# Weight blocks A for batches 0 and 1, then B for 1 and 0, with a second buffer of split inputs that attention fills directly

## The chip, the cores and the metric

The kernel runs on one core of a Trainium2 chip. The metric is the device time of one execution in microseconds (us), the median of several runs. In the texts below PE is TensorE (matmul), ACT is ScalarE, DVE is VectorE, SP is SyncE, which here only issues DMAs.

## What is computed

Three stages follow each other, all in float32, over 4 batches of 8 heads, 512 local and 32 global positions, 64 columns a head.

```
k_all, v_all = concat(k_g, k_l), concat(v_g, v_l)
out_g = softmax(q_g k_all^T / 8) v_all                      # 32 global rows see everything
out_l = softmax([q_l k_g^T / 8, band(q_l k_l^T / 8)]) v_all  # 512 local rows: global + |i-j| <= 32
x = concat(out_g, out_l) -> (4*544, 512)
x = (silu(x @ w_gate) * (x @ w_val)) @ w_out                # 512 -> 1536 -> 512: "layer 1"
h = x @ w_in;  x = (max(h,0) + alpha*min(h,0)) @ w_out2     # 512 -> 2048 -> 512: "layer 2"
```

The weights arrive as pairs of float32 words read as 64-bit integers, so each block has to be taken apart on the chip.

## The kernel before

Everything that TensorE does in the two layers runs on numbers split into a high and a low part, each of a rounded 32-bit type: three matmuls (high·high, high·low, low·high) stand for one. `mm12` (line 460) is such a product over a contraction of 512: 4 pieces by 3 passes, 12 matmuls. `xa` holds the split inputs of layer 1 and later of layer 2.

**Attention** is cut into 40 units (`Local`: two heads, 256 query rows; `Global`: four heads), 4 steps each, run by `apump` (line 317): scores on PE, masked minimum on DVE, exponentials on ACT (`s`), division on DVE (`n`), transposes on PE with a copy by ACT (`t`), the product with V on PE and its copy out (`pv`). A step of one unit stands beside steps of its neighbours, so a unit's chain is spread over three rounds. In the opening stretch a step may use any of 8 PSUM banks; afterwards only the two banks `a0` and `a1` (line 651). `pv` writes batch 0's result split into `xa` (two instructions, lines 222 and 223); of batches 1 to 3 it writes the result unsplit into `yp` or `y3`, by one ACT copy (line 219).

**Weights.** `wload` issues the DMA of a block, `wpump` converts one in seven instructions: lines 407, 408 and 424 on ACT (424 in some cases as line 422 on DVE), lines 409, 410, 413 and 388 on DVE. The 36 blocks of layer 1 (12 slices `f` of gate, value and out) are split once, written back to HBM as `w1s`, and read again as `w<-w1s` when they are wanted a second time. SBUF holds 18 blocks of layer 1: the half GA (f 0 to 5) or the half GB (f 6 to 11). `reload` queues the blocks of the other half one by one as those of this half are used for the last time.

**Visits.** `visit1(b, c0, c1, fs, ...)` runs columns c0 to c1 of batch b through one half of the slices: per slice 12 matmuls for gate (`ps_g`), 12 for value (`ps_v`), 12 for out (`ps_acc`). Before the first visit 24 attention steps run with no layer work beside them (the opening). The order then is, with the short names used below:

- 0a: batch 0, columns 0 to 255, GA; 0b: batch 0, columns 256 to 511, GA
- 0GB, 1GB, 1GA, 2GA, 2GB: a whole batch (512 columns) through one half
- 3: batch 3 and the global rows, in four visits; then layer 2 in five chunks (`visit2`)

What interleaves them is `pump()`: called several times in a visit, it starts `wrate` weight loads, takes one conversion step, and runs attention steps until their count has reached its share of a target (`pumper`: `nslots` calls to reach `target`). So the numbers ns0 to ns3 say how thickly attention stands in each visit, and ws1 how many weight loads go with each step of the opening. At the end of a visit `xprep` splits the next batch's `yp` into `xa` (`yprep`), and the same is done between the chunks of layer 2, by `boundary`.

The recording layer then places each engine's instructions in an order of its own from the program order and dependencies, so that neighbours in the code may stand some places apart on an engine.

Of the kernel before, what the change touches and what calls it, by code (L numbers as in the profile page):

```python
# [39 lines left out]
def kernel(  # L40
# [303 lines left out]
    st["w"], st["lo"] = 0, 0  # L344
# [4 lines left out]
    def dbl_tile():  # L349
        i = ring["d"] = (ring["d"] + 1) % ND  # L350
        if i == 2 and st["k"] < mark[3] - 4:
            return const.tile([128, 512], I64, tag="y30", name="dblx")
# [42 lines left out]
    def wpump():  # L395
# [60 lines left out]
    def xprep(b):  # L456
        assert st["k"] >= mark[b + 1] + LAG
        yprep(b, 0, S)

    def mm12(o, w, c0, c1):  # L460
# [96 lines left out]
    def yprep(b, c0, c1):  # L557
        for k in range(4):
            if (c0, c1) == (0, S) and b < B - 1:
                src = yp[b][:, :, k]  # L560
                hi, lo = (xa[:, i, k, 0:S].rearrange("p (a c) -> p a c", a=2) for i in range(2))
                with pr("xp"):
                    nc.scalar.activation(out=hi, in_=src, func=ACTF.Copy)
                    nc.vector.tensor_tensor(out=lo, in0=src, in1=hi, op=ALU.subtract)
                continue
            for src, o, z in ypieces(b, c0, c1):
                hi, lo = xa[:, 0, k, o:o + z], xa[:, 1, k, o:o + z]
                nc.scalar.activation(out=hi, in_=src(k), func=ACTF.Copy)
                nc.vector.tensor_tensor(out=lo, in0=src(k), in1=hi, op=ALU.subtract)
# [8 lines left out]
    def visit2(b, c0, c1, pump, late, alpha, boundary=None):  # L578
# [15 lines left out]
        for f in range(NF2):  # L594
# [33 lines left out]
    if True:  # L628
# [95 lines left out]
        chunks = [(0, 0, 512), (1, 0, 512), (2, 0, 512), (3, 0, 384), (3, 384, 640)]  # L724
        for i, (b, c0, c1) in enumerate(chunks):
            nx = chunks[i + 1] if i + 1 < len(chunks) else None
            visit2(b, c0, c1, p, late, alpha, boundary=(lambda nx=nx: yprep(*nx)) if nx else None)
# [84 lines left out]
```

## Time and profile before

| | |
|---|---|
| runs | 988.06 us median of 3 (986.29 to 989.24) |
| the profiled execution | 986.18 us; its span, first to last instruction, 984.4 us |
| PE busy | 965.3 us (98%), mean granted clock 0.989 |
| ACT busy, DVE busy | 488.2 us (50%), 522.3 us (53%) |
| DMA | 103.43 MB, 105 GB/s over the span |

A busy share over the whole span hides that the first fifth and the rest are different: in the first 175 us ACT and DVE are busy nine tenths of the time, afterwards a quarter to a half. PE's matmuls are pipelined and their ends are modelled, so PE reads as busy even where it advances slowly; the number of matmuls that a stretch holds says more. The rows below are therefore cut at the borders of the visits.

### The profile page before, as it was taken

The page shows a single profiled execution, that of the slowest core. Times are in us where ns is not written, and L with a number is a line of the kernel's source. Part 1 is how long each engine was busy: PE and PEld are TensorE (multiplying, and loading weights), DVE is VectorE, ACT ScalarE, POOL GpSimd, SP SyncE. Part 2 cuts the span into 40 slices and gives each one's busy share as a digit, 9 for nine tenths or more (in the row PEclk, how much of TensorE's full clock was granted, in tenths as well). Part 3 has the DMA queues.
Part 4 walks back from the last instruction along what each step waited for, and adds up shares of the span by engine and source line. Part 5 has one row for each costly group of instructions (what it writes and reads, how often), then busy time and mean ns, then how long its engine had stood idle before and what let it go on. Part 6 is the DMA issues. An engine that isn't in the chain of part 4 may idle for free.

```text
span 984.4 us, 14324 instructions
## 1 busy us (share of the span) xinstructions
PE 965.3 (98%) x5556; PEld 801.5 (81%) x5556; DVE 522.3 (53%) x1247; ACT 488.2 (50%) x983; POOL 0.7 (0%) x6
## 2 busy tenths in 40 slices
PE   7899999999999999999999999999999999999998
PEld 5678887777777777778999998888888888899897
DVE  6889888553323443325941279944434543444453
ACT  7899999755565655653532155523222322322322
POOL 0000000000000000000000000000000000000000
PEclk9699999999999999999999999999999999999999
DMA  8979795425421034401368033200100100010000
GB/s 262 321 260 338 230 345 161 172 70 182 148 90 50 28 103 132 150 1 55 120 207 254 10 108 129 86 1 1 43 1 1 43 1 1 0 43 1 8 26 21
DMA packets 33683, 103.43 MB, mean 105 GB/s; under 512 B 3920, under 2 KB 8016, under 8 KB 33616
## 3 DMA queue, kind: packets, MB, share of 16 engines
q1 hardware_dynamic: 33616, 102.53, 31.5%
q8 instruction: 43, 0.70, 0.3%
q14 instruction: 24, 0.20, 0.1%
HBM read 79.18 MB, written 23.33 MB: 104 GB/s over the span
## 4 chain that ended last, share of the span: by engine, by line
PE 83%; DVE 7%; ACT 5%; DMA 4%; issue 1%; SPq 0%; ACTq 0%; DVEq 0%
PE ps_acc L590 19%; PE ps_g L466 17%; PE ps_v L466 16%; PE ps_acc L499 10%; PE ps_a L466 9%; PE ps_a L157 3%; DMA dbl<-in_w_dram 3%; PE ps_a L211 3%; PE ps_a L203 2%; DVE raw L413 1%; DVE dbl L410 1%; PE ps_a L240 1%; PE ps_a L283 1%; DVE w L388 1%; ACT e L183 1%
## 5 line engine op out<-in xcount | busy, mean ns | idle before, releaser
L466 PE MATMUL ps_g<-xa,w 128*128 128x512 f32 (+2 forms) x1032 | 210.6, 352 | 0.9 <-ACT sg L513 0.9
L466 PE MATMUL ps_v<-xa,w 128*128 128x512 f32 (+2 forms) x1032 | 208.9, 351 | 0.5 <-DVE w L388 0.5
L466 PEld LDWEIGHTS ps_g<-xa,w 128*128 128x128 f32 x1032 | 168.9, 190 | 30.2 <-issue 8.4
L466 PEld LDWEIGHTS ps_v<-xa,w 128*128 128x128 f32 x1032 | 169.1, 190 | 24.9 <-issue 4.7
L590 PE MATMUL ps_acc<-w,h 128*128 128x512 f32 x561 | 138.2, 392 | 0.2 <-DVE h L609 0.2
L590 PEld LDWEIGHTS ps_acc<-w,h 128*128 128x128 f32 x561 | 104.5, 188 | 22.5 <-DVE h L609 0.6
L499 PE MATMUL ps_acc<-h,w 128*128 128x512 f32 (+2 forms) x600 | 119.5, 351 | 0.0
L499 PEld LDWEIGHTS ps_acc<-h,w 128*128 128x128 f32 x600 | 97.4, 189 | 15.2 <-issue 2.7
L522 DVE TENSOR_TENSOR t<-ps_v,sg 128x512 f32<-128x512 f32 (+1 forms) x54 | 35.7, 660 | 124.0 <-PE ps_v L466 106.1
L466 PE MATMUL ps_a<-xa,w 128*128 128x512 f32 (+2 forms) x480 | 100.8, 359 | 0.0
L466 PEld LDWEIGHTS ps_a<-xa,w 128*128 128x128 f32 x480 | 83.5, 188 | 13.4
L170 DVE CUSTOM_DVE_ANT_0 e<-ps_a,lm 128x256 f32<-128x256 f32 x112 | 41.7, 421 | 56.8 <-PE ps_a L157 56.5
L183 ACT ACTIVATE e<-e,mx 128x256 f32<-128x256 f32 x128 | 63.7, 499 | 14.9 <-DVE mx L170 13.8
L608 ACT ACTIVATE h<-g 128x512 fp32r<-128x512 f32 (+2 forms) x55 | 31.3, 568 | 74.4 <-DVE g L607 74.4
L590 PE MATMUL ps_acc<-w,hx 128*128 128x512 f32 x255 | 63.1, 394 | 0.0
L604 DVE TENSOR_SCALAR g<-ps_a,alpha 128x512 f32<-128x512 f32 (+2 forms) x40 | 26.8, 671 | 57.6 <-ACT r L603 57.1
L590 PEld LDWEIGHTS ps_acc<-w,hx 128*128 128x128 f32 x255 | 47.5, 188 | 10.4
L513 ACT ACTIVATE sg<-ps_g 128x512 f32<-128x512 f32 (+1 forms) x54 | 31.0, 574 | 46.4 <-PE ps_g L466 46.1
L513 ACT ACT_TABLE_LOAD x30 | 38.5, 1283 | 28.6 <-PE ps_g L466 28.3
L603 ACT ACTIVATE r<-ps_a 128x512 f32<-128x512 f32 (+2 forms) x40 | 21.2, 531 | 59.0 <-PE ps_a L466 58.6
L609 DVE TENSOR_TENSOR h<-g,h 128x512 fp32r<-128x512 f32 (+2 forms) x55 | 33.7, 612 | 31.1 <-ACT h L608 31.0
L607 DVE TENSOR_TENSOR g<-g,r 128x512 f32<-128x512 f32 (+2 forms) x80 | 48.9, 611 | 2.4
(123 smaller groups left out, 1071.9 us busy)
## 6 DMA issues: line engine op xcount, KB each, us to landing
w<-w1s SPq DMA_DIRECT2D x54, 512.0 KB, 3.6
dbl<-in_w_dram SPq DMA_DIRECT2D x50, 512.0 KB, 4.0
w1s<-w SPq DMA_DIRECT2D x36, 512.0 KB, 5.2
qk<-in_qk_dram SPq DMA_DIRECT2D x12, 592.0 KB, 5.8
dblx<-in_w_dram SPq DMA_DIRECT2D x9, 512.0 KB, 5.6
yp<-in_w_dram SPq DMA_DIRECT2D x9, 512.0 KB, 6.1
out_dram<-o SPq DMA_DIRECT2D x16, 256.0 KB, 2.0
v<-in_v_dram SPq DMA_DIRECT2D x12, 320.0 KB, 4.2
```

The source lines that it names most:

```text
L157: nc.tensor.matmul(out=s[h][:, 256 * i:256 * i + 256], lhsT=x[rows, WIN + 128 * t:WIN + 128 * t + 128], rhs=x[rows, 128 * t:128 * t + 256] ...
L170: nc.vector.tensor_tensor_reduce(out=self.e[:, j], in0=s[h][:, 256 * i:256 * i + 256], in1=lm[:, 2 * self.half + i], scale=-0.125, scalar= ...
L183: nc.scalar.activation(out=self.e[:, j], in_=self.e[:, j], func=ACTF.Exp, scale=-1.0, bias=mx[:, j:j + 1], accum_out=self.sm[:, j:j + 1],)
L211: nc.tensor.matmul(out=o[D * h:D * h + D, c0:c1], lhsT=v[:, h, kt + d], rhs=self.pt[:, h, x:x + c1 - c0], start=(i == 0), stop=(i == 2),)
L466: nc.tensor.matmul(out=o, lhsT=a, rhs=x, start=(i == 0), stop=(i == 11))
L499: nc.tensor.matmul(out=acc[m][:, 0:n], lhsT=a, rhs=x, start=(f == fs[0] and j == 0), stop=(f == fs[-1] and j == 2),)
L513: nc.scalar.activation(out=sg[:, 0:nn], in_=g[:, 0:nn], func=ACTF.Silu)
L522: nc.vector.tensor_tensor(out=t[:, 0:nn], in0=v[:, 0:nn], in1=sg[:, 0:nn], op=ALU.mult)
L590: nc.tensor.matmul(out=acc[t], lhsT=a, rhs=x, start=(i == 0 and j == 0), stop=(i == NF2 - 1 and j == 2))
L607: nc.vector.tensor_tensor(out=g[:, 0:n], in0=g[:, 0:n], in1=r[:, 0:n], op=ALU.add)
L608: nc.scalar.activation(out=h[:, 0, 0:n], in_=g[:, 0:n], func=ACTF.Copy)
L609: nc.vector.tensor_tensor(out=h[:, 1, 0:n], in0=g[:, 0:n], in1=h[:, 0, 0:n], op=ALU.subtract)
```

## The change

- The order of visits becomes 0a, 0b, then 1GA, 1GB, 0GB, 2GB, 2GA, and in 3 the halves are swapped. GA so serves batches 0 and 1 before GB is wanted at all, and layer 1's blocks are read back from HBM in two visits and no longer in three.
- A second buffer `xb` (16 KB a partition) holds split inputs. `pv` writes every batch's result split, batches 0 and 3 into `xa`, 1 and 2 into `xb`; `xprep` goes, and so does the unsplit copy. Room for it comes from a smaller scratch for DMA descriptors (`dynamic_dma_scratch_size=1024`).
- Layer 2's chunks alternate between `xb` and `xa`; the next chunk's inputs are split during slices 4, 6, 8 and 10 of this one (`ahead`) and no longer at its end.
- All attention of batch 1 now has to be done before 1GA, so it is packed into 0b (15 calls of `pump` where 27 were shared by 0b and 0GB). 1GA and 1GB have nearly none; batch 2's stands in 0GB (18 calls), batch 3's in 2GB and 2GA. In 0a and 0b `pump` is also called between the two slices of a group.
- In the opening ws1 falls from 0.4 to 0.2 weight loads a step.

```
-    HEAT=20, ws0=1.0, ws1=0.4, ND=4, NR=5, NQ=4, LAG=8,
+    HEAT=20, ws0=1.0, ws1=0.2, ND=4, NR=5, NQ=4, LAG=8,
-    ns0=7, ns1=27, ns2=35, ns3=32, e0=8, ...
+    ns0=14, ns1=15, ns2=34, ns3=18, ns4=34, e0=8, ...
+    xb = const.tile([128, 2, 4, 512], F32R, name="xb")
+    xof = (xa, xb, xb, xa)
...
-            if self.pair.b:
-                evac(yh(self.pair.b, hf)[:, p], o[:, 0:256], "ye")
-                return
-            hi, lo = (xa[:, i, p, 256 * hf:256 * hf + 256] for i in range(2))
+            hi, lo = (xof[self.pair.b][:, i, p, 256 * hf:256 * hf + 256] for i in range(2))
             nc.scalar.activation(out=hi, in_=o[:, 0:256], func=ACTF.Copy)
             nc.vector.tensor_tensor(out=lo, in0=o[:, 0:256], in1=hi, op=ALU.subtract)
...
             for q, f in enumerate(gf):
-                mm12(g[:, n * q:n * q + n], weight((1, f, "g")), c0, c1)
+                mm12(g[:, n * q:n * q + n], weight((1, f, "g")), xof[b], c0, c1)
+                if q + 1 < len(gf):
+                    pump()
...
-        visit1(0, 256, 512, GA, False, p, after_f=reload(GB, GA), third=early)
-        visit1(0, 0, 512, GB, True, p, boundary=lambda: xprep(1), third=early)
...
-        visit1(1, 0, 512, GB, False, p, after_f=reload(GA, GB), third=early)
-        visit1(1, 0, 512, GA, True, p, boundary=lambda: xprep(2))
...
-        visit1(2, 0, 512, GA, False, p, after_f=reload(GB, GA))
-        visit1(2, 0, 512, GB, True, p, boundary=lambda: xprep(3))
+        visit1(0, 256, 512, GA, False, pumper(P["ns1"], mark[2] + P["e1"], P["wr1"], P["g1"]), third=early)
+        assert st["k"] >= mark[2] + LAG
+        p = pumper(P["ns2"], mark[2] + 11, P["wr2"])
+        visit1(1, 0, 512, GA, False, p, after_f=reload(GB, GA), third=early)
+        visit1(1, 0, 512, GB, True, p, third=early)
+        assert st["k"] <= mark[2] + 11
+        st["ph"] = 1
+        visit1(0, 0, 512, GB, True, pumper(P["ns3"], mark[3] + 11, 1.0, P["g2"]), third=early)
+        assert mark[3] + LAG <= st["k"] <= mark[3] + 11
+        p = pumper(P["ns4"], mark[4] + P["e3"], P["wr3"], P["g3"])
+        visit1(2, 0, 512, GB, False, p, after_f=reload(GA, GB))
+        visit1(2, 0, 512, GA, True, p)
...
+        chunks = [(xb, 0, 0, 512), (xa, 1, 0, 512), (xb, 2, 0, 512), (xa, 3, 0, 384), (xb, 3, 384, 640)]
+        for k in range(4):
+            yprep(k, *chunks[0])
+        visit1(3, 256, 640, GB, True, p, after_f=more, third=late)
...
+            if ahead and f in (4, 6, 8, 10):
+                ahead(f // 2 - 2)
```

How the instructions move shows at three places. The first is ACT in the opening, between the copies of the third and the fourth unit's transposes (`pt<-...`; `e` are the exponentials, `raw`, `dbl`, `dblx`, `w` and `yp` belong to weight conversions). Before:

```order
27 L407 ACTIVATE raw<-dbl 128x512
28 L408 ACTIVATE dbl<-dbl 128x512
29 L183 ACTIVATE e,sm<-e,mx 128x256 x2
30 L222 ACTIVATE xa<-ps_acc_443 128x256
31 L183 ACTIVATE e,sm<-e,mx 128x256
32 L424 ACTIVATE w<-raw 128x512
33 L183 ACTIVATE e,sm<-e,mx 128x256 x2
34 L407 ACTIVATE raw<-dblx 128x512
35 L408 ACTIVATE dblx<-dblx 128x512
36 L140 ACTIVATE pt<-ps_acc_418 128x512
```

and in the changed program:

```order
24 L185 ACTIVATE e,sm<-e,mx 128x256
25 L423 ACTIVATE w<-yp_95 128x512
26 L185 ACTIVATE e,sm<-e,mx 128x256
27 L221 ACTIVATE xa<-ps_acc_407 128x256
28 L185 ACTIVATE e,sm<-e,mx 128x256 x2
29 L406 ACTIVATE yp_95<-dbl 128x512
30 L407 ACTIVATE dbl<-dbl 128x512
31 L185 ACTIVATE e,sm<-e,mx 128x256 x2
32 L142 ACTIVATE pt<-ps_acc_384 128x512
```

Three conversion pieces now stand between them instead of five; over the whole opening ACT starts 5 blocks and finishes 4, where it started 8 and finished 7.

The second place is PE at the end of 0b, in the matmuls into `ps_acc` (`h` and `hx` are the products of gate and value; `qk`, `pt`, `ptg`, `ident` mark attention). Before:

```order
207 L466 MATMUL ps_v<-xa,w 128x256 x24
208 L203 MATMUL ps_a_1532<-ident,e 128x128 x4
209 L499 MATMUL ps_acc_1176<-h,w 128x256 x3
210 L499 MATMUL ps_acc_1177<-h,w 128x256 x3
211 L499 MATMUL ps_acc_1178<-h,w 128x256 x3
212 L499 MATMUL ps_acc_1179<-h,w 128x256 x3
```

and in the changed program:

```order
286 L213 MATMUL ps_a_1758<-pt,v 64x256 x2
287 L213 MATMUL ps_a_1758<-pt,v 64x128 x4
288 L159 MATMUL ps_a_1767<-qk 128x256 x2
289 L494 MATMUL ps_acc_1179<-h,w 128x256
290 L159 MATMUL ps_a_1768<-qk 128x256 x2
291 L205 MATMUL ps_a_1785<-ident,e 128x128 x4
292 L494 MATMUL ps_acc_1179<-h,w 128x256 x2
293 L494 MATMUL ps_acc_1180<-h,w 128x256 x3
294 L205 MATMUL ps_a_1807<-ident,e 128x128 x4
295 L282 MATMUL ps_a_1820<-ptg,v 64x32 x20
296 L494 MATMUL ps_acc_1177<-hx,w 128x256 x2
297 L159 MATMUL ps_a_1843<-qk 128x256 x2
```

Before, the 72 matmuls at the end of 0b stand in one run; now attention steps cut into them.

The third is PE just behind 0b: before, the start of 0GB, now the start of 1GA. Before:

```order
237 L466 MATMUL ps_g<-xa,w 128x512 x12
238 L274 MATMUL ps_a_1692<-ident,sg 128x128 x4
239 L466 MATMUL ps_v<-xa,w 128x512 x12
240 L274 MATMUL ps_a_1733<-ident,sg 128x128
241 L211 MATMUL ps_a_1754<-pt,v 64x256 x2
242 L211 MATMUL ps_a_1754<-pt,v 64x128 x4
```

and in the changed program:

```order
307 L494 MATMUL ps_acc_1180<-hx,w 128x256 x3
308 L205 MATMUL ps_a_1942<-ident,e 128x128 x4
309 L461 MATMUL ps_g<-xb,w 128x512 x12
310 L461 MATMUL ps_v<-xb,w 128x512 x12
311 L461 MATMUL ps_g<-xb,w 128x512 x12
```

Layer work with attention between every group has become layer work alone, for two whole visits.

## Rows read from the trace of the kernel before

**Rows 1.** The page's busy times, whole span.

```profile
PE 965.3 (98%) x5556; PEld 801.5 (81%) x5556; DVE 522.3 (53%) x1247; ACT 488.2 (50%) x983; POOL 0.7 (0%) x6
```

**Rows 2.** Windows at the visits: opening, 0a, 0b, 0GB, 1GB, 1GA, 2GA, 2GB.

```profile
core 0: us, PE busy (x) PEld busy (x) DVE busy (x) ACT busy (x) POOL busy (x), PEclk, DMA share, GB/s
0.00:40.50 40.50, 29.81 (x157) 20.62 (x157) 31.12 (x109) 30.90 (x80) 0.70 (x6) 0.80 0.88 293
40.50:97.40 56.90, 54.95 (x460) 45.34 (x460) 50.63 (x153) 51.10 (x111) 0.00 (x0) 0.96 0.84 295
97.40:135.80 38.40, 37.45 (x310) 33.31 (x309) 33.25 (x81) 37.12 (x75) 0.00 (x0) 1.00 0.83 279
135.80:212.10 76.30, 76.30 (x474) 57.23 (x474) 55.12 (x163) 62.31 (x130) 0.00 (x0) 1.00 0.48 167
212.10:278.70 66.60, 66.60 (x388) 51.08 (x386) 19.53 (x64) 35.15 (x67) 0.00 (x0) 1.00 0.53 163
278.70:346.30 67.60, 67.60 (x399) 51.49 (x398) 27.43 (x94) 40.58 (x85) 0.00 (x0) 1.00 0.11 36
346.30:416.20 69.90, 69.90 (x413) 52.43 (x411) 24.11 (x83) 40.90 (x80) 0.00 (x0) 1.00 0.41 128
416.20:474.60 58.40, 58.37 (x332) 46.05 (x331) 28.43 (x67) 29.85 (x58) 0.00 (x0) 1.00 0.14 46
```

**Rows 3.** The chain in order of time, pieces of PE alone: start us, us, what.

```profile
340.06 5.62 PE ps_acc L499 x24
385.82 2.97 PE ps_acc L499 x12
448.40 2.72 PE ps_v L466 x12
538.83 2.86 PE ps_g L466 x24
613.85 2.81 PE ps_a L466 x12
647.19 2.72 PE ps_v L466 x12
```

**Rows 4.** Windows of 10 us in the opening, columns as in Rows 2.

```profile
0.00:10.00 10.00, 7.89 (x44) 6.07 (x44) 2.99 (x18) 4.33 (x12) 0.70 (x6) 1.00 0.80 237
10.00:20.00 10.00, 7.54 (x43) 4.79 (x42) 9.00 (x29) 9.33 (x24) 0.00 (x0) 1.00 0.86 304
20.00:30.00 10.00, 8.22 (x42) 5.28 (x41) 9.03 (x33) 8.11 (x23) 0.00 (x0) 0.54 0.92 297
30.00:40.00 10.00, 5.67 (x32) 4.22 (x31) 9.60 (x33) 8.63 (x24) 0.00 (x0) 0.67 0.96 335
```

**Rows 5.** Groups by line on DVE and ACT, 0 to 212 us.

```profile
L410 DVE SCALAR_TENSOR_TENSOR dbl<-dbl 128x512 int32<-128x512 int32 x23 | 15.7, 687 | 2.2 <-ACT dbl L408 2.0
L388 DVE TENSOR_TENSOR w<-raw,w 128x512 fp32r<-128x512 f32 x22 | 15.0, 684 | 0.2 <-ACT w L424 0.2
L409 DVE TENSOR_SCALAR raw<-raw 128x512 f32<-128x512 f32 x25 | 10.5, 422 | 1.0 <-ACT raw L407 1.0
L413 DVE SCALAR_TENSOR_TENSOR raw<-raw,dbl 128x512 int32<-128x512 int32 x13 | 8.9, 686 | 0.0
L424 ACT ACTIVATE w<-raw 128x512 fp32r<-128x512 f32 x18 | 11.3, 630 | 1.3 <-DVE raw L413 1.2
L408 ACT ACTIVATE dbl<-dbl 128x512 int32<-128x512 uint32 x23 | 15.4, 676 | 1.6 <-DMA dbl<-in_w_dram 1.6
```

**Rows 6.** ACT in order of time, around a table load.

```profile
100.97 1.28 ACT L513 ACT_TABLE_LOAD   x1
102.27 0.60 ACT L513 ACTIVATE sg<-ps_g 128x512 f32<-128x512 f32 x1
```

**Rows 7.** Issues of DMA by SP: times, size, median us to landing.

```profile
w<-w1s SPq DMA_DIRECT2D x54, 512.0 KB, 3.6
```

**Rows 8.** What PE waited for, whole span: us, times, longest.

```profile
PE ps_acc L590 <- DVE h L609: 0.2, 1, 0.2
```

More of the change, by code (lines that the diff above doesn't have):

```diff
@@ L343 @@
     wloaded, wsplit, wlo = deque(), [], deque()
-    st["w"], st["lo"] = 0, 0
+    st["w"], st["ph"] = 0, 0
     w1s = [dram.tile([128, 3, 2, 512], F32, name=f"w1s{f}") for f in range(NF1)]
@@ L350, in dbl_tile @@
         i = ring["d"] = (ring["d"] + 1) % ND
-        if i == 2 and st["k"] < mark[3] - 4:
+        if i == 2 and not st["ph"]:
             return const.tile([128, 512], I64, tag="y30", name="dblx")
-        if i == 3 and st["k"] < mark[2] - 4:
+        if i == 3 and not st["ph"]:
             return yp[2][:, 1].rearrange("p m c -> p (m c)").bitcast(I64)
@@ L358, in raw_tile @@
         i = ring["r"] = (ring["r"] + 1) % NR
-        if i >= 3 and st["k"] < mark[2] - 4:
+        if i >= 3 and not st["ph"]:
             return yp[2][:, 0, 2 * (i - 3):2 * (i - 3) + 2].rearrange("p m c -> p (m c)")
@@ L398, in wpump @@
         wlow()
-        while wloaded and wloaded[0][3] <= st["w"] - (P["wl0"] if st["k"] < mark[4] else P["wl1"]):
+        while wloaded and wloaded[0][3] <= st["w"] - (P["wl1"] if st["ph"] == 2 else P["wl0"]):
             e = wloaded.popleft()
@@ L454, in passes, with mm12 @@
         return ((a[0], b[0]), (a[0], b[1]), (a[1], b[0]))
[L456 to L460, printed above, removed]
+    def mm12(o, w, xs, c0, c1):
         i = 0
@@ L463, in mm12 @@
             wk = [w[:, p, 128 * k:128 * k + 128] for p in range(2)]
-            xk = [xa[:, p, k, c0:c1] for p in range(2)]
+            xk = [xs[:, p, k, c0:c1] for p in range(2)]
             for a, x in passes(wk, xk):
@@ L480, in early, with visit1 @@
         return const.tile([128, 2, 512], F32R, tag="y31", name="hx")
-    def visit1(b, c0, c1, fs, last, pump, after_f=None, boundary=None, third=None):
+    def visit1(b, c0, c1, fs, last, pump, after_f=None, third=None):
         n = c1 - c0
@@ L516, in visit1 @@
             for q, f in enumerate(gf):
-                mm12(v[:, n * q:n * q + n], weight((1, f, "v")), c0, c1)
+                mm12(v[:, n * q:n * q + n], weight((1, f, "v")), xof[b], c0, c1)
                 if after_f:
                     after_f(f, "gv")
+                if q + 1 < len(gf):
+                    pump()
             t = work.tile([128, 512], F32, tag="t", name="t")
@@ L555, in visit1, with yprep @@
                         nc.scalar.activation(out=dst(m), in_=acc[m][:, o:o + z], func=ACTF.Copy)
[L557 to L569, printed above, removed]
+    def yprep(k, x, b, c0, c1):
+        for src, o, z in ypieces(b, c0, c1):
+            hi, lo = x[:, 0, k, o:o + z], x[:, 1, k, o:o + z]
+            nc.scalar.activation(out=hi, in_=src(k), func=ACTF.Copy)
+            nc.vector.tensor_tensor(out=lo, in0=src(k), in1=hi, op=ALU.subtract)
     def out_rows(b, c):
@@ L576, with visit2 @@
     cnt = {"u": 0}
-    def visit2(b, c0, c1, pump, late, alpha, boundary=None):
+    def visit2(x, b, c0, c1, pump, late, alpha, ahead=None):
         n = c1 - c0
@@ L597, in visit2 @@
             cnt["u"] += 1
-            mm12(u[:, 0:n], weight((2, f, "i")), 0, n)
+            mm12(u[:, 0:n], weight((2, f, "i")), x, 0, n)
             r = work.tile([128, 512], F32, tag="sg", name="r")
@@ L705 @@
             want_w2(f, q, wx)
+        st["ph"] = 2
         p = pumper(1, 0, P["wr4"])
-        visit1(3, 0, 256, GB, False, p, third=late)
-        visit1(3, 256, 640, GB, False, p, after_f=reload(GA, GB), third=late)
-        visit1(3, 0, 256, GA, True, p, third=late)
+        visit1(3, 0, 256, GA, False, p, third=late)
+        visit1(3, 256, 640, GA, False, p, after_f=reload(GB, GA), third=late)
+        visit1(3, 0, 256, GB, True, p, third=late)
         nxt = [12]
@@ L718 @@
         p = pumper(1, 0, P["wr5"])
-        visit1(3, 256, 640, GA, True, p, after_f=more, boundary=lambda: yprep(0, 0, 512), third=late)
+        chunks = [(xb, 0, 0, 512), (xa, 1, 0, 512), (xb, 2, 0, 512), (xa, 3, 0, 384), (xb, 3, 384, 640)]
+        for k in range(4):
+            yprep(k, *chunks[0])
+        visit1(3, 256, 640, GB, True, p, after_f=more, third=late)
         yp0p.release()
@@ L723 @@
         want_w2(*order[-1], wy)
[L724 to L727, printed above, removed]
+        for c, nx in zip(chunks, chunks[1:] + [None]):
+            visit2(*c, p, late, alpha, ahead=(lambda k, nx=nx: yprep(k, *nx)) if nx else None)
         wy.release()
```

11 lines of the change are left out of this document (2 added, 9 removed).

## The prediction

> **What bounds the kernel now.** I read the busy times first: PE is busy 98% of the span, the other engines half of it [rows 1], so only work on PE, or time in which PE cannot advance, can move the end. Busy time does not tell the two apart, because matmuls are pipelined. So next come the windows cut at the visits, with the number of matmuls in each [rows 2], and the chain's pieces for what a group of matmuls takes where nothing disturbs it [rows 3]: 12 matmuls of 512 columns take 2.72 us (227 ns each), 24 of 256 columns 2.86 us (119 ns each).
>
> Every visit has 216 matmuls of layer 1, so 216 x 0.119 = 25.7 us in 0a and 0b, 216 x 0.227 = 49.0 us in the others. What is left of each window, divided by its other matmuls, is the price of an attention matmul there, waits included:
>
> - 0a: 56.9 - 25.7 = 31.2 us for 460 - 216 = 244, 128 ns; 0b: 12.7 us for 94, 135 ns
> - 0GB: 27.3 us for 258, 106 ns; 1GB 17.6 for 172, 102; 1GA 18.6 for 183, 102; 2GA 20.9 for 197, 106. Together 84.4 us for 810, 104 ns
> - 2GB: 9.4 us for 116, 81 ns
>
> So PE is the bound from about 136 us on, and attention costs 104 ns a matmul there. Before that it costs a quarter more, in visits where ACT is busy 90% (0a) and 97% (0b) of the time [rows 2]; and in the opening PE has nothing but attention, while DVE is busy 9.0 to 9.6 of every 10 us from the tenth on [rows 4]. What there is to win lies in the first 136 us.
>
> **The change part by part.**
>
> Layer work: the same 216 matmuls a visit, 7 visits and batch 3; nothing is removed from PE. Counted over PE's whole new order, with the two records that the trace has for a matmul on half the array, attention matmuls stand as follows: 0a 245 (244 before), 0b 347 (94), 1GA 4, 1GB 16, 0GB 346, 2GB 177, 2GA 113. PE turns from layer work to attention 121 times (117 before). So attention is moved, not saved, and the question is its price at the new places.
>
> 0b: 25.7 us + 347 matmuls. Both ends are prices of before: 104 ns (undisturbed) gives 36.1, 135 ns (0b as it was) gives 46.8. Which one is nearer is told by ACT. In 0a ACT is busy 51.1 us; 11 blocks are finished there, each with three instructions of 0.63 to 0.68 us [rows 5], 1.98 us together, so 21.8 us; the other 29.3 us go with 244 attention matmuls, 0.120 us each. For 0b that makes 347 x 0.120 + 10 pieces of conversions that its order holds (6.7 us) = 48 us, in a visit of some 65 us: 74%, like 0GB (62.3 of 76.3, 82%, price 106) and not like 0a. But steps stand more thickly than in any visit before, 347 in 65 us against 258 in 76, through two PSUM banks. I take 115 ns: 39.9, so 65.6 us.
>
> 1GA and 1GB: 98.0 us + 20 x 0.104 = 100.1 us. GB's conversion lies beside them: 18 blocks, on DVE 0.42 + 3 x 0.69 = 2.48 us each [rows 5], 44.6 us, on ACT 35.6 us, against 100 us of PE; the layer work of such a visit with its attention keeps DVE busy 19.5 us of 66.6 (1GB) [rows 2]. PE costs nothing as long as a block is ready when its slice comes; if one is late, PE waits out at most what is left of one conversion, some 2.5 us.
>
> 0GB: 49.0 + 346 x 0.104 = 85.0 us. No conversion is left for it. 2GB: 49.0 + 177 x 0.104 = 67.4. 2GA takes the place of the last visit of before, with 113: 49.0 + 113 x 0.081 = 58.2.
>
> Sum from the end of 0a to batch 3: 65.6 + 100.1 + 85.0 + 67.4 + 58.2 = 376.3 us, against 474.6 - 97.4 = 377.2 before: -0.9 us. What GB's conversions no longer disturb is eaten by the thicker attention in 0b.
>
> Opening and 0a: three blocks fewer are converted in the opening, 3 x 2.48 = 7.4 us of DVE on the engine that holds it, and three more in 0a. At the end of 0a the same 18 blocks are done and the same attention, so DVE has its 31.1 + 50.6 = 81.7 us in either case. 3.0 of them lie in the first 10 us [rows 4], when it waits for input; the other 78.7 took 87.4 us. At the density of the best row (9.60 of 10) they take 82.0: -5.4 us at best. At worst the opening keeps its length, because the chain and not DVE's load holds it, and 0a pays the three blocks: +7.4. The finer calls of `pump` in 0a speak for a better density; I take half of the best, -2.7 us.
>
> What goes at the visits' ends: PE does not stand there now, the 24 matmuls over the end of 1GA take 5.62 us, 234 ns each [rows 3], while `xprep` runs. So dropping `xprep` gives nothing, neither does the second buffer by itself; the additional low part per local unit goes to a DVE that is busy 29 to 72% of the time in these visits. Before layer 2 PE waited 0.2 us for a product [rows 8]: -0.2, as inputs are split a visit earlier. 18 of the 54 reads of `w1s` go [rows 7]; DMA is busy 0.11 to 0.53 there [rows 2], and no row has PE waiting for them: 0. SP issues its loads in one queue with the stores of converted blocks, and that queue only gets shorter.
>
> Sum: -0.9 - 2.7 - 0.2 = -3.8 us. The profiled execution took 986.18 us (a span of 984.4 and 1.8 us around it), so 982.4. It lies 1.9 us below the median of the three runs, from which the same step gives 984.3. I forecast **984 us**.
>
> A rule of the Trainium skill speaks against packing 0b. First the row: a table load takes 1.28 us on ACT and the next activation starts 0.02 us behind it [rows 6]. The page "ScalarE: Activation LUTs", section "What ACT_TABLE_LOAD costs", puts a drain of about 1.38 us on top, 2.66 us a switch. By the rule the 6 loads in 0b would keep ACT 8.3 us longer, 56 of 65 us, so 0b would pay 0a's 128 ns: 4.5 us more, and the sum would be +0.7 instead of -3.8. The trace does not agree with the drain.
>
> **Rivals.**
>
> *Attention stalls in 0b (slower).* With only a0 and a1, each step needs the copy or reduction of the step before last. If 0b pays its old 135 ns, it costs 6.9 us more than I take; if 0GB, where steps stand as thickly per group, pays 0a's 128 ns, 8.3 more: -3.8 + 15.2 = +11.4, from the median 999 us. It decides from 126 ns in 0b on, where the gain is gone; 135 alone makes the kernel slower by 3 us. For it: 244 matmuls in 57 us already cost 128 in 0a. Against it: that price came with ACT at 90%, and 0GB paid 106 at 82%.
>
> *The opening wins fully (clearly faster).* 0a ends 5.4 us earlier; 0b pays 104 (-3.8); steps of 0GB and 2GB that stand together share the turn from layer work to attention (a group takes 2.97 us before a turn and 2.72 without [rows 3]) and pay 2GB's 81 ns: 523 x 0.023 = -12.0. That is -3.8 - 2.7 - 3.8 - 12.0 = -22; half of the last is more likely: -16, from the median 972 us. Against it: the number of turns does not fall.
>
> *Tiles in other places (little or slower).* In layer 2 the same 12 matmuls take 2.81 us in early slices and 2.72 in later ones of a chunk [rows 3], with the weights in another pool and nothing waited for. `xb` moves nearly all tiles. If its products come out at 2.81, the 80 groups that read it (24 in 1GA and 1GB, 24 for batch 2, 32 in layer 2) pay 80 x 0.09 = 7.2 us: 991.5 us.
>
> *Table loads drain.* A mechanism that no row shows; with the switches in 0b at twice their length the time would be 988 to 989.
>
> **How the numbers follow.** This kernel can tell a change from none at about 0.3%, 3 us: faster is below 985.1, slower above 991.0. Chances: the forecast 0.48, with a range of its own of 977 to 990 (faster 0.26, same 0.20, slower 0.02); stalls in 0b 0.24 (slower 0.22, same 0.02); the full win 0.18, all faster; other places 0.08 (same 0.04, slower 0.04); the drain 0.02, same. Together faster 0.44, same 0.28, slower 0.28. The range reaches into both outer cases without their ends: 968 to 998 us.
>
> **What would show it.** Right, if in the new profile 0a ends between 92 and 98 us, 0b takes 62 to 69 us, 1GA and 1GB about 50 us each with groups of 2.72 us, 0GB about 85, and batch 3 starts near 471 us. Wrong in the opening, if 0a ends later than 100; wrong in 0b, if its attention matmuls cost 126 ns or more; the places of tiles are at work, if 1GA's groups take 2.8 us with no wait in front of them. A layer 2 that is longer than before by over 2 us would make the whole sum wrong, as I let it be.

## The result, and the profile after

The changed kernel took **1000.0 us** (median of 4 runs, 997.39 to 1002.25), the one before 987.7 us beside it: a ratio of 1.0126, 95% interval 1.0108 to 1.0143. I had forecast 984 us, in a range of 968 to 998: wrong, in the direction too. The profiled execution took 1000.49 us with a span of 998.7, against 986.18 and 984.4.

The page's busy times of the kernel after answer to [rows 1]:

```profile
PE 975.5 (98%) x5556; PEld 809.7 (81%) x5556; DVE 526.4 (53%) x1265; ACT 458.7 (46%) x961; POOL 0.7 (0%) x6
```

PE has as many instructions as before and is as full; ACT has 29.5 us less to do. So the matmuls themselves take longer, or PE stands. The windows of the kernel after, cut at its visits, answer to [rows 2], with the columns of that group: opening, 0a, 0b, 1GA, 1GB, 0GB, 2GB, 2GA, and last the first two visits of batch 3.

```profile
0.00:33.00 33.00, 25.30 (x157) 17.60 (x157) 25.03 (x99) 25.20 (x71) 0.70 (x6) 0.96 0.88 291
33.00:96.30 63.30, 58.71 (x463) 47.49 (x463) 54.79 (x158) 56.27 (x123) 0.00 (x0) 0.94 0.84 298
96.30:164.60 68.30, 67.89 (x564) 53.64 (x564) 44.09 (x165) 51.62 (x131) 0.00 (x0) 1.00 0.29 100
164.60:214.20 49.60, 49.60 (x224) 41.07 (x223) 38.30 (x71) 30.63 (x52) 0.00 (x0) 1.00 0.77 265
214.20:267.40 53.20, 51.67 (x233) 41.53 (x232) 18.42 (x29) 14.84 (x26) 0.00 (x0) 1.00 0.21 70
267.40:356.40 89.00, 89.00 (x563) 64.45 (x562) 41.71 (x154) 54.37 (x123) 0.00 (x0) 1.00 0.13 43
356.40:424.30 67.90, 67.90 (x394) 51.37 (x394) 23.60 (x81) 37.03 (x75) 0.00 (x0) 1.00 0.43 132
424.30:482.70 58.40, 58.40 (x332) 46.08 (x331) 25.52 (x61) 27.00 (x53) 0.00 (x0) 1.00 0.10 33
482.70:552.50 69.80, 66.09 (x434) 65.78 (x433) 33.98 (x62) 24.65 (x49) 0.00 (x0) 0.95 0.61 193
```

The same two visits of batch 3 before:

```profile
474.60:538.70 64.10, 63.60 (x434) 63.28 (x433) 29.76 (x53) 21.95 (x44) 0.00 (x0) 1.00 0.65 199
```

The forecast for this execution was 982.4 us; it is missed by 18.1 us, which fall on: batch 3's first two visits 5.7 (69.8 against 64.1, not in my sum at all), 0GB 4.0 (89.0 against 85.0), 0b 2.8 (68.4 against 65.6), 1GB 2.5 (53.2 against 49.0 + 16 x 0.104), opening and 0a 1.6 (96.3 against 97.4 - 2.7), all else 1.5. 1GA, 2GB and 2GA stand where they were forecast, within 0.5 us. Two of these terms come again in other profiles (0GB 89.0 in e1 and e4, 0b 68.4 in e1 and e8, experiments below). The others differ from one profile to the next: batch 3's first two visits took 66.0 to 69.8 us in five profiles, 0a ended at 93.1 in e1, and 1GB took 51.1 there.

**Batch 3.** PE in order of time there (start us, us, what; in brackets idle time and what ended it):

```profile
508.55 2.25 PE L461 MATMUL ps_g<-xa,w 128*128 128x384 f32 x12
510.64 2.24 PE L461 MATMUL ps_v<-xa,w 128*128 128x384 f32 x12
516.59 4.21 PE L461 MATMUL ps_g<-xa,w 128*128 128x384 f32 x12 [3.71 <-ACT sg L510]
520.59 2.91 PE L461 MATMUL ps_v<-xa,w 128*128 128x384 f32 x12
```

ACT in the same stretch:

```profile
511.63 0.66 ACT L406 ACTIVATE raw<-dbl 128x512 f32<-128x512 f32 x1 [2.89 <-DMA dbl<-in_w_dram]
512.19 0.91 ACT L552 ACTIVATE y<-ps_acc 128x256 f32<-128x256 f32 x3
512.98 0.67 ACT L407 ACTIVATE dbl<-dbl 128x512 int32<-128x512 uint32 x1
515.50 0.65 ACT L407 ACTIVATE dbl<-dbl 128x512 int32<-128x512 uint32 x1 [1.85 <-DMA dbl<-in_w_dram]
516.06 0.47 ACT L510 ACTIVATE sg<-ps_g 128x384 f32<-128x384 f32 x1
```

The gate product is finished near 510.8 us. Its silu (`sg`) starts at 516.06, because conversion pieces of layer 2's first blocks stand ahead of it in ACT's queue and wait there for their DMA. Loads and conversions take turns in the chain: a load of 4.42 us from 502.72, its conversion, then a load of 5.41 us from 509.99, which is issued when the conversion has freed its buffer. `ps_g` is not free for the next group, and PE stands for 3.71 us. Then twelve matmuls of 384 columns take 4.0 us, where 2.08 is their time otherwise (from 523.50 us on). The windows behind the wait show why (columns as above; the last but two is the granted clock):

```profile
516.60:520.60 4.00, 4.00 (x13) 4.00 (x14) 1.91 (x4) 0.52 (x1) 0.00 (x0) 0.50 0.44 114
520.60:523.40 2.80, 2.80 (x14) 2.80 (x14) 0.69 (x1) 1.16 (x2) 0.00 (x0) 0.75 0.97 363
```

After the wait PE runs at 1.2 GHz, half of 2.4, for some 5 us: 1.9 + 0.7 us more. Undisturbed, these visits take 63.3 us (e1, below). So the kernel after loses 6.5 here, 3.7 of it waiting and 2.6 by the clock; the one before lost 0.8.

**0GB.** PE in order of time, columns as above:

```profile
299.69 1.13 PE L159 MATMUL ps_a<-qk 64*128 64x256 f32 x4
300.75 0.50 PE L494 MATMUL ps_acc<-h,w 128*128 128x512 f32 x1
301.18 1.13 PE L159 MATMUL ps_a<-qk 64*128 64x256 f32 x4
302.24 1.89 PE L494 MATMUL ps_acc<-h,w 128*128 128x512 f32 x7
```

Line 159 is the score matmul of a `Local` unit. Each head uses half of the array's rows and a PSUM bank of its own. Each matmul on half the array has two records, so a head's two matmuls have four. Four records of one head take 1.06 us (299.69 to 300.75), four of the other 1.06 again. Where the order leaves all eight together they take 1.06 to 1.07 in all (e8, below): the heads run side by side. A unit whose heads the order has pulled apart pays 1.06 us twice. That the order does so because one of the two banks came free earlier is my reading of it. Counted over PE's records from 0a to batch 3, 6 units have other matmuls between their heads before (4 in 0a, 2 in 0GB), 16 after (4 in 0a, 6 in 0b, 4 in 0GB, and one over each end of 0GB). The 9 and 20 of the expectations below count the opening too (3 and 4).

Score matmuls alone in 0GB of the kernel after (line 159; PE and PEld with their counts, then the last three columns as above):

```profile
267.40:356.40 89.00, 14.64 (x65) 8.75 (x64) 1.00 0.13 43
```

That each head must have its own bank is stated in the Trainium skill ("TensorEngine Tiling (Array Packing)", "Restrictions and Gotchas"): row tiles write to different banks and cannot share one at a time. No run here put both in one bank.

**1GB.** The chain, pieces in order of time:

```profile
218.55 6.10 DMA dbl<-in_w_dram
225.30 0.67 ACT dbl L407
225.97 0.52 ACT h L525
227.02 3.02 PE ps_g L461 x12
230.03 2.72 PE ps_v L461 x12
232.75 2.72 PE ps_acc L494 x12
```

and PE's row behind it:

```profile
227.02 3.02 PE L461 MATMUL ps_g<-xb,w 128*128 128x512 f32 x12 [1.06 <-ACT sg L510]
```

It is batch 3's mechanism once more: a DMA at the head of ACT's queue, layer work behind it. PE stands 1.5 us in this visit for it, 0.47 at 220.23 us and 1.06 here. Behind it the groups that read `xb` take 2.72 us as in [rows 3], so the places of the tiles cost nothing.

### The profile page after: what moved, and what is told of

It is laid out like the page before. It is cut to its first block, busy times and chain, and to the rows that moved or that the text cites. A ratio compares the mean times of both kernels' runs of the same rounds, so it can differ in the third digit from the quotient of the medians.

```text
span 998.7 us, 14304 instructions
## 1 busy us (share of the span) xinstructions
PE 975.5 (98%) x5556; PEld 809.7 (81%) x5556; DVE 526.4 (53%) x1265; ACT 458.7 (46%) x961; POOL 0.7 (0%) x6
## 4 chain that ended last, share of the span: by engine, by line
PE 80%; DMA 8%; ACT 5%; DVE 5%; issue 1%; SPq 1%; ACTq 0%
PE ps_acc L579 19%; PE ps_g L461 15%; PE ps_v L461 14%; PE ps_acc L494 10%; PE ps_a L461 9%; DMA dbl<-in_w_dram 6%; PE ps_a L159 4%; PE ps_a L213 3%; PE ps_a L205 2%; DMA yp<-in_w_dram 1%; PE ps_a L282 1%; ACT dbl L407 1%; DVE raw L412 1%; PE ps_a L239 1%; DVE w L387 1%
## 5 line engine op out<-in xcount | busy, mean ns | idle before, releaser
L461 PE MATMUL ps_g<-xa,w 128*128 128x256 f32 (+2 forms) x600 | 111.5, 332 | 5.8 <-ACT sg L510 5.6
L461 PE MATMUL ps_v<-xa,w 128*128 128x256 f32 (+2 forms) x600 | 110.9, 331 | 0.0
L461 PEld LDWEIGHTS ps_g<-xa,w 128*128 128x128 f32 x600 | 93.9, 192 | 18.6 <-ACT sg L510 6.1
L461 PE MATMUL ps_g<-xb,w 128*128 128x512 f32 (+1 forms) x432 | 100.9, 382 | 1.5 <-ACT sg L510 1.5
L461 PEld LDWEIGHTS ps_v<-xa,w 128*128 128x128 f32 x600 | 94.7, 194 | 8.8 <-issue 4.0
L461 PE MATMUL ps_v<-xb,w 128*128 128x512 f32 (+1 forms) x432 | 100.2, 381 | 0.0
L461 PEld LDWEIGHTS ps_g<-xb,w 128*128 128x128 f32 x432 | 77.3, 188 | 19.2 <-ACT sg L510 2.4
L461 PEld LDWEIGHTS ps_v<-xb,w 128*128 128x128 f32 x432 | 77.5, 188 | 16.8 <-issue 1.7
L185 ACT ACTIVATE e<-e,mx 128x256 f32<-128x256 f32 x128 | 63.8, 500 | 26.8 <-DVE mx L172 26.2
L461 PE MATMUL ps_a<-xb,w 128*128 128x512 f32 (+1 forms) x288 | 59.4, 355 | 0.0
L593 DVE TENSOR_SCALAR g<-ps_a,alpha 128x512 f32<-128x512 f32 (+2 forms) x40 | 26.8, 670 | 60.7 <-ACT r L592 60.2
L461 PEld LDWEIGHTS ps_a<-xb,w 128*128 128x128 f32 x288 | 48.5, 188 | 8.7
```

Of the source, the lines that this page charges most:

```text
L185: nc.scalar.activation(out=self.e[:, j], in_=self.e[:, j], func=ACTF.Exp, scale=-1.0, bias=mx[:, j:j + 1], accum_out=self.sm[:, j:j + 1],)
L593: nc.vector.tensor_scalar(out=g[:, 0:n], in0=u[:, 0:n], scalar1=0.0, scalar2=alpha[:, f:f + 1], op0=ALU.min, op1=ALU.mult)
```

## The experiments

Each was timed beside the kernel before (987.3 to 987.8 us); the ratios are to it. The visits' times are from one profile each.

**e1: attention ends sooner.**

```
-    ns0=14, ns1=15, ns2=34, ns3=18, ns4=34, ...
+    ns0=14, ns1=15, ns2=34, ns3=18, ns4=30, ...
```

> One number is changed in the kernel after: ns4 is 30 and no longer 34, so the attention steps of 2GB and 2GA come sooner and the last of them stands 108 matmuls of layer work ahead of batch 3 (60 in the kernel after, 84 in the kernel before). Theory A (batch 3 starts too close behind attention: the first 12 blocks of layer 2 are converted when attention's memory is free, and the last of these conversions, waiting for their DMA at the head of ACT's queue, hold up the silu of batch 3's second visit): PE's waits of 7.1 us for sg in that visit go, the first two visits of batch 3 lose some 5 to 6 us, and the kernel takes about 994.5 to 995.5 us. Rival B (the waits come from the swapped halves of batch 3 or from the blocks themselves, not from where attention ends): no change within 1 us, 999 to 1001 us. Rival C (thicker attention in 2GB and 2GA costs as much as is won): batch 3 gains its 5 us, 2GB and 2GA take 3 us or more longer than 67.9 and 58.4.

Measured 996.9 us, ratio 1.0092 (1.0067 to 1.0118). The window of batch 3's first two visits:

```profile
479.10:542.40 63.30, 63.30 (x433) 63.27 (x432) 25.45 (x48) 19.01 (x38) 0.00 (x0) 1.00 0.59 184
```

63.3 us and no idle PE. Theory A holds for the place; B falls. (The 7.1 us that I quoted are all waits for `sg`: 3.7 of them lie here, 1.9 in 0a, 1.5 in 1GB.) Of C some is true: 2GB and 2GA together take 128.0 instead of 126.3, and what follows these visits up to the last matmul 443.5 instead of 441.4, with a wait of 1.6 us for `hx` that the kernel after does not have. So less than 3 of the 6.5 us are left, near the 3.1 us between the medians and under the 4.5 to 5.5 that A forecast. In five profiles with ns4 34 these visits of batch 3 took 66.0 to 69.8 us, in six with 30 or 32 always 63.3.

**e2 and e3: the two heads tied**, in the kernel after and in the kernel before.

```
-                for h in range(2):
+                for h in (1, 0):
...
-                    nc.tensor.matmul(
+                    mm = nc.tensor.matmul(
...
+                    if (i, h) != (0, 1):
+                        tc.keep_in_program_order(mm)
```

The last line keeps a matmul right behind the one before it in PE's order.

> The kernel after, with the score matmuls of the two heads of a local unit (rows 0 to 63 and 64 to 127 of the array, one PSUM bank each) tied: the one whose bank comes free second is issued first, and the other three follow right behind it in PE's order. Theory D (a pair of heads that the order separates costs 1.06 us more, because the two half-array matmuls no longer run side by side; 20 units are separated in the kernel after, 9 in the kernel before, and that is most of what 0b and 0GB cost above the forecast): the records of these matmuls stand at 133 ns each everywhere, 0GB comes down by some 4 us from 89.0, 0b with the part of 1GA that takes its last steps by some 5 from 117.9 together, the kernel by 6 to 12 us, to 988 to 994. Rival E (the separated halves only fill time in which PE would wait for a PSUM bank anyway): the halves run side by side, but PE waits for the banks instead, and the time stays within 2 us of 1000, or gets worse as the first step waits for both banks.

> The same tie of the two heads' score matmuls in the kernel before, where 9 units are separated: 3 in the opening, 4 in 0a, 2 in 0GB. Theory D: at most 2 us in 0GB and some of 4 us in 0a, which ACT and DVE bound in part, so 983 to 986 us, and the two kernels come closer to each other by some 6 us. Rival E: within 2 us of 988, as in the kernel after.

e2 took 996.8 us (1.0068 to 1.0109), e3 992.9 us (1.0030 to 1.0065): the kernel after gained some 3 us, the one before lost 5. In e2, 0GB fell from 89.0 to 85.7, as D has it; 0b and 1GA together only from 117.9 to 116.8: no pair is apart there any more, but PE is idle 4.0 us of the 116.8, where it was 0.4. In e3 the loss lies in opening and 0a, which end at 105.8 instead of 97.4 us, and 0GB, with two pulled-apart units, gained nothing (78.3 us with 266 attention matmuls, 76.3 with 258). Up to the end of 0a PE is idle 21.7 us in e3, before 12.6. So D holds for 0GB of the kernel after. Elsewhere the tie costs waits on PE about what it saves, or more, as E has it.

**e8: the tie from 0GB on only.** The same edit, for steps from `mark[2] + 11` on.

> The kernel after with the two heads' score matmuls tied only for the units that begin in 0GB or later; everything ahead of 0GB is as in the kernel after. Theory D: 0GB alone gets shorter, from 89.0 to 85.5 to 86 us (the 5 separated units, some 1.06 us each, less what the wait for the second bank takes), the kernel takes 996 to 998 us. Rival E: 0GB stays within 1 us of 89.0.

994.5 us (1.0048 to 1.0095), 1.5 us under D's range. 0GB, then its score matmuls alone:

```profile
262.30:348.10 85.80, 85.42 (x565) 60.17 (x563) 41.76 (x154) 54.96 (x123) 0.00 (x0) 1.00 0.13 45
```

```profile
262.30:348.10 85.80, 9.08 (x64) 5.51 (x64) 1.00 0.13 45
```

In PE's order of time the two heads stand together:

```profile
290.78 1.13 PE L159 MATMUL ps_a<-qk 64*128 64x256 f32 x8
...
298.56 1.14 PE L159 MATMUL ps_a<-qk 64*128 64x256 f32 x8
```

No unit is pulled apart, and attention costs (85.7 - 49.0) / 346 = 106 ns a matmul, the price of 0GB before. The score matmuls take 5.6 us less than in the kernel after (14.64 and 9.08), and 0GB gets 3.3 us shorter; where the other 2.3 went is not shown. So 3.3 us of 0GB's 4.0 are shown; what the run gained besides lies in batch 3 (66.0) and 0a (60.7), which the tie does not touch and which vary between executions.

**e7: ns4 at 30, and the tie from batch 2's first unit on.**

> The kernel after with ns4 at 30, and with the two heads' score matmuls tied as in the run e2, but only for units of batches 2 and 3 and the end of batch 1, so that opening and 0a are as in the kernel after. Theories A and D together: 0GB takes 85.5 to 86 us instead of 89.0, batch 3's first two visits 63 to 64 instead of 69.8, sum 990 to 993 us. If the tie's gain in 0GB was one of the opening's order and not of the tie: 0GB stays at 89 and the kernel at 996 to 997 us.

989.6 us (1.0009 to 1.0037): 0GB 85.8, batch 3's visits 63.3, both as expected, the time 0.4 us under the range.

**e5: four banks for attention in 0a and 0b.**

```
+        duo = [bank(f"acc{m}") for m in range(2)] if b == 0 and n == 256 else None
...
+                    nc.tensor.matmul(out=d, lhsT=zero, ..., start=True, stop=False)
...
-        att_tags["list"] = ["a0", "a1"]
+        att_tags["list"] = ["a0", "a1", "acc2", "acc3"]
```

> The kernel after, with four PSUM banks for attention in 0a and 0b instead of two: in these visits, whose sums are 256 columns wide, two of the four sums share a bank (a matmul with zeros over 512 columns opens each pair, 0.2 us, and one copy of 512 columns replaces two of 256), and acc2 and acc3 go to attention. From 1GA on nothing is changed. Theory S (the forecast's rival: with two banks each step waits for the copy of the step before last, and 0b pays 123 ns for an attention matmul for that reason): hardly a pair of heads is separated any more in 0b, its attention comes to 105 to 110 ns a matmul, 0b takes 62 to 64 us instead of 68.4, 0a loses 2 us or more, and the kernel takes 991 to 995 us. Rival T (0a and 0b are held by ACT and DVE, which convert 18 blocks beside attention): 0a and 0b keep their 63.3 and 68.4 us within 1.5, the kernel stays at 998 to 1001.

997.4 us (1.0072 to 1.0130), between the two forecasts. 0b:

```profile
101.90:165.70 63.80, 63.06 (x552) 50.15 (x551) 43.48 (x165) 49.77 (x126) 0.00 (x0) 1.00 0.32 102
```

(63.8 - 25.7) / 333 = 114 ns instead of 123. So 0b gains what S says, and through the pairs. The score matmuls of 0b alone, in the kernel after and in e5 (columns as for 0GB):

```profile
96.30:164.60 68.30, 16.34 (x64) 9.87 (x64) 1.00 0.29 100
101.90:165.70 63.80, 12.01 (x64) 7.09 (x64) 1.00 0.32 102
```

They take 4.3 us less, and 0b is 4.6 us shorter. In the kernel after one of 0b's eight units takes 1.06 us, one 1.60 and six, pulled apart, 2.12; in e5 five take 1.06 to 1.13, one 1.68 and two 2.12. The waits for a bank that S names are not what 0b paid: in the kernel after PE is idle 0.4 us of its 68.3. 0a took 66.9 us instead of 63.3, at a clock of 0.90, so a gain from four banks in 0a is not shown, as T has it there.

**e4 and e6: ws1**, back to 0.4 in the kernel after, and 0.2 alone in the kernel before.

> The kernel after with one part undone: ws1 is 0.4 weight loads a step in the opening again, and no longer 0.2. Theory F (what the shorter opening wins, 0a pays: the same blocks are converted by the end of 0a in either case): the opening takes 7 us more and 0a 5 to 7 us less, 0a ends within 2 us of 96.3, and the kernel takes 999 to 1002 us. Rival G (the opening was 7.5 us shorter for nothing, as 0a is the visit that steps on two PSUM banks slow down, not its conversions): 0a stays at 63 us, ends near 103, and the kernel takes 1006 us.

> The kernel before with one part of the change alone: ws1 is 0.2 weight loads a step in the opening and no longer 0.4. Theory F2 (the part is worth what the kernel after with 0.4 showed, some 4 us at the end of 0a, as DVE and ACT convert three blocks beside matmuls and no longer ahead of them): the opening ends near 33 us, 0a at 93 to 94 instead of 97.4, the kernel takes 983.5 to 985.5 us. Rival (it pays only with the finer calls of pump in 0a, which the kernel before does not have): 0a ends at 97 or later, 987 to 991 us.

e4 took 1004.0 us (1.0140 to 1.0186), e6 989.6 (1.0006 to 1.0030). Opening and 0a of e4:

```profile
0.00:42.20 42.20, 30.89 (x157) 21.01 (x157) 31.14 (x109) 31.00 (x80) 0.70 (x6) 0.89 0.86 282
42.20:100.30 58.10, 54.86 (x460) 45.09 (x459) 50.56 (x146) 52.48 (x114) 0.00 (x0) 0.96 0.84 297
```

and of e6:

```profile
0.00:35.40 35.40, 27.27 (x157) 19.21 (x157) 25.25 (x99) 25.18 (x71) 0.71 (x6) 0.88 0.87 283
35.40:100.30 64.90, 59.95 (x459) 48.41 (x459) 54.22 (x156) 53.72 (x117) 0.00 (x0) 0.91 0.76 258
```

ws1 moves the border of the two stretches by 5 to 9 us and the end of 0a by 3 to 4. In e4 0a gave back 5.2 of the opening's 9.2 us, so F is right about the exchange and 2 us off at its end; G falls. 0.2 pays 4 us in the kernel after and costs 2 in the one before: F2 falls, and the time is the one of its rival. That the finer calls of `pump` make the difference is not shown, as no run has them alone, and the end of 0a differs by 3 us between executions of the same instructions (96.3 and 93.1).

**e9, e10, e11: together.** ns4 30, the tie from 0GB on, four banks in 0b alone; then wl1 3 besides; then, instead, ns4 32.

> The kernel after with ns4 at 30, the tie from 0GB on, and four PSUM banks for attention in 0b alone (0a keeps its two). Theories A, D and S: batch 3's first two visits 63 to 64 us (69.8), 0GB 85.5 to 86 (89.0), 0b 63.5 to 64.5 (68.4), 0a at 61 to 64, sum 983 to 987 us, so at or under the kernel before. Rival T (what 0b gains with four banks stands in 0a or 1GA again, as in the run with four banks in both): 1GA begins at 164 us or later and the kernel takes 988 to 991 us.

> The kernel of e9 with wl1 at 3 and no longer 2: from batch 3 on a conversion stands one call of pump later behind the load that it waits for. Theory A2 (what is left of the waits from batch 3 on, 1.6 us of PE for hx and 0.4 behind it in the last visit of batch 3, comes from conversions at the head of ACT's queue that wait for their DMA): batch 3 and layer 2 together take 1 to 3 us less than in e9. Rival: the loads are held by their two buffers and come a call later too, no change within 1 us, or a weight block of layer 2 comes late and it gets 1 to 5 us slower.

> The kernel of e9 with ns4 at 32: the last attention step stands 84 matmuls of layer work ahead of batch 3, as in the kernel before. Theory A: batch 3's first two visits take 63.5 to 65 us (64.1 in the kernel before), 2GB and 2GA together 1 us less than with 30, the kernel within 1.5 us of e9. Rival B2 (84 matmuls are enough before only by the other order of the halves): 66 us or more for the first two visits, and the kernel 2 to 3 us above e9.

987.7 us (0.9989 to 1.0021), 987.7 (0.9994 to 1.0017) and **986.7 us** (0.9980 to 1.0015). All three are level with the kernel before; no version beats it. e9 is 0.7 us over its forecast. 0b keeps its gain (1GA begins at 159.7 to 161.7 us): with about as many attention matmuls in 0b as in the kernel after, 350, it takes 64.2 to 64.3 us, (64.3 - 25.7) / 350 = 110 ns, and in e9 and e11 its score matmuls take 12.1 us. So S holds for 0b in size, and T does not. wl1 gives nothing: batch 3's first two visits take 63.3 us in both, what follows them 443.0 against 441.4. With ns4 32 these visits take 63.3 as well, so B2 falls. 0a, 0b, 1GB, 0GB and batch 3's visits in e11:

```profile
34.30:95.40 61.10, 56.91 (x459) 45.84 (x459) 54.85 (x158) 55.61 (x122) 0.00 (x0) 0.96 0.86 305
95.40:159.70 64.30, 63.60 (x571) 51.55 (x569) 43.07 (x166) 50.66 (x130) 0.00 (x0) 1.00 0.33 109
...
209.20:261.50 52.30, 50.73 (x230) 40.91 (x228) 17.99 (x28) 13.94 (x24) 0.00 (x0) 1.00 0.22 71
261.50:347.20 85.70, 85.33 (x564) 60.12 (x562) 41.75 (x154) 54.96 (x123) 0.00 (x0) 1.00 0.13 45
...
474.00:537.30 63.30, 63.30 (x433) 63.30 (x432) 29.73 (x55) 21.72 (x44) 0.00 (x0) 1.00 0.63 198
```

Against the kernel after: batch 3 -6.5, 0b -4.1, 0GB -3.3, 1GB -0.9, opening and 0a -0.9, 2GB and 2GA +0.4; together -15.3, and the spans differ by 15.2 (998.7 and 983.5).

**e12 and e13: write-backs out of 0a.**

```
+                if key[1] < NF1 // 2:
+                    held.append((key, t))
...
+        for _ in range(2 if st["k"] >= mark[1] + P["e0"] else 0):
...
+                tc.keep_in_program_order(
+                    nc.sync.dma_start(out=w1s[key[1]][:, "gvo".index(key[2])], in_=t.bitcast(F32)))
```

GA's blocks are held, instead of being stored at once, and go out two a call of `pump` in 0b.

> The kernel of e11 (ns4 32, tie from 0GB on, four banks in 0b), with the 18 write-backs of GA's split blocks (512 KB each, 9.4 MB) held until 0b, two a call of pump, behind everything that SP has issued. In 0b the changed kernel's DMA is busy 0.29. Theory M (DMA holds 0a: the share is over 1 at 70 to 80 us, loads take 7.5 to 10 us there instead of 5, PE waits and its clock falls): 0a takes 57 to 59 us instead of 61.2 to 63.3, its clock stays at 1.0, 1GA begins at 154 to 157 us, the kernel takes 981 to 984 us and beats both. Rival N (ACT and DVE hold it): 0a keeps 60.5 to 63 us although its DMA share falls to some 0.65, the kernel stays at 985 to 988.

> The kernel before with the same 18 write-backs held until 0b, where GB's blocks are loaded, converted and written back already (DMA share 0.83 in 0b). Theory M: 0a gets 2 to 4 us shorter than 56.9, but 0b pays 9.4 MB more at some 280 GB/s and gets 2 us or more longer than 38.4, so the kernel stays within 2 us of 987.3: the change, which left 0b without conversions, is what makes room. Rival N: 0a stays at 56 to 57 us, 0b gets longer all the same, 988 to 992 us.

988.5 us (0.9996 to 1.0022) and 987.5 us (0.9993 to 1.0021): M falls. In e13 0a took 57.7 us, and 0b 37.3, though both theories had it longer than the 38.4 of before. 0a of e12:

```profile
33.90:99.80 65.90, 60.86 (x458) 49.66 (x459) 55.39 (x163) 57.60 (x124) 0.00 (x0) 0.87 0.65 219
```

0a of e1, then of e8:

```profile
32.40:93.10 60.70, 55.80 (x462) 44.70 (x463) 55.22 (x160) 56.10 (x123) 0.00 (x0) 1.00 0.89 316
```

```profile
32.70:93.40 60.70, 55.67 (x461) 44.60 (x462) 55.21 (x160) 56.04 (x123) 0.00 (x0) 1.00 0.88 313
```

The DMA share falls to 0.65 and 0a gets no shorter; its time goes with the granted clock instead (60.7 us at 1.00, 61.1 at 0.96 in e11, 63.3 at 0.94 in the kernel after, 63.0 at 0.93 in e9, 65.0 at 0.89 in e10, 65.9 at 0.87). At a clock of 1.00 ACT is busy 56.0 of 60.7 us, so N is the nearer theory; that ACT is the bound there was not tested. What else 0a would need to get under 60 us was not tried.

## Why the prediction was wrong

- **"Sum from the end of 0a to batch 3"** is the step that failed by most in the profiled execution. It ends at batch 3, and I took what follows 2GA as unchanged, with no row for it. The conversion of layer 2's blocks begins where attention's memory comes free, and that was moved: from 84 matmuls of layer work ahead of batch 3 to 60. Against the 64.1 us of before it cost 1.9 to 5.7 us in five profiles, so that the profiled execution shows the worst of them. With 84 or 108 matmuls in front the changed kernel's visits take 63.3 us (e11, e1). The order showed the distance before any run; I counted attention per visit in it and not where its last step stands.
- **"0GB: 49.0 + 346 x 0.104 = 85.0 us"**: a price from visits with 169 to 258 attention matmuls, used for 346. Measured 116 ns; 106 with the heads kept together (e8). The mechanism was right, that attention is moved and its price at the new place decides; what failed is the size of that price, because an order through two banks pulls pairs apart (in 0GB the tie was tried, four banks in 0b alone).
- **"I take 115 ns"** for 0b: 123. With four banks 114 (e5); in e9 to e11 it is 110. So the rival "attention stalls in 0b" had the right place, the two PSUM banks, but neither its size nor its mechanism: together with 0GB 6.8 us, where I had put 15.2; its point of decision (126 ns) was not reached; and PE did not wait for a copy, it ran the two heads of a unit one after the other. The six units that are apart, at 1.06 us each, are 6.4 us, as much as 123 ns is above 104 over 347 matmuls (6.6 us). ACT at 51.6 of 68.3 us was no bound in 0b, as I had argued.
- **"PE costs nothing as long as a block is ready"** in 1GA and 1GB: right for 1GA (49.5). 1GB paid 2.5 us, which only by chance is the bound that I had named and set to 0: 1.5 of it is waiting, for a silu behind a conversion and not for a block. In ten other profiles of the changed kernel's versions 1GB took 50.1 to 53.0 us, most of them with 1GB as it was, so it varies from one execution to the next.
- **"I take half of the best, -2.7 us"** for opening and 0a: -1.1 in this profile, -4.3 in e1's with the same instructions up to there. My size lies between the two, but they are 3.2 us apart, more than the term itself, so that is luck. The reason failed where it was tried: with three blocks fewer in the opening alone the kernel before ends 0a 2.9 us later (e6).
- Right: 2GB and 2GA; tiles in other places (groups of 2.72); layer 2 (441.4 us with batch 3's last two visits, 440.9 before, up to the last matmul). That dropping `xprep` and reading `w1s` less gives nothing fits these visits; no run has either alone.
- The full win did not come: 2GB still paid (67.9 - 49.0) / 177 = 107 ns and 0GB more; PE turns to attention 121 times, before 117.

## What to carry to other kernels

When a change moves work, price also the stage that starts when the moved work ends, and count in the order how much cover is left in front of it. Work packed twice as thickly through the same two buffers does not keep its price; look in the order for pairs of instructions that run side by side and are pulled apart. An in-order queue that mixes prefetch work with the work of the loop passes a late DMA on to the loop: here one wait of 3.7 us became 6.3.

## What the hardware showed that I had not expected

- Score matmuls on half of the array's rows: 8 records of two heads together take 1.06 us, 4 of one head alone take 1.06 us as well; keeping pairs together made 0GB 3.3 us shorter, and four banks, with five of 0b's eight pairs together instead of one, made 0b 4.1 us shorter (e9 to e11).
- After a wait of 3.71 us PE ran at half its clock for some 5 us, 2.6 us on top of the wait. In e8 PE was idle 2.1 us in the same two visits, and their mean clock stayed at 1.00. In 0a a wait of 1.9 us for silu at 69.8 us was followed by a mean clock of 0.66 from 70 to 80 us in the kernel after; in e1 the same instructions stood 2.0 us at 68.9 us and the clock stayed at 1.00. The two windows, after and e1:

```profile
70.00:80.00 10.00, 9.76 (x51) 8.04 (x51) 8.48 (x26) 8.29 (x19) 0.00 (x0) 0.66 1.02 398
```

```profile
70.00:80.00 10.00, 9.72 (x71) 8.02 (x70) 9.54 (x28) 9.13 (x21) 0.00 (x0) 1.00 1.02 404
```

That is 51 matmuls against 71 in 10 us. What decides between the two is open.
